# Attention front end of a fused kernel: heads grouped as 4 g + j, logits copied out of PSUM with the read-out, scores scaled as they are copied out, one tile for two sets of sums

## The chip, the cores and the metric

The kernel runs on one core of a Trainium2 chip. The metric is the device time of one execution in microseconds (us); three runs of the kernel before stand as its reference. The trace of one profiled execution gives every instruction's start and duration on TensorE (PE; PEld is its weight load), VectorE (DVE), ScalarE (ACT) and GpSimd (POOL); SP issues most of the DMA transfers, each engine's own queue is written with a q (SPq).

## The reference

Three parts follow one another: an attention between 512 tokens and 32 state rows in both directions, a mixture of experts with one expert per token, and a bilinear layer. Only the first is edited:

```
x: (B=8, H=8, S=512, D=64)   state: (8, 8, 32, 64)   scale = 1/8
xread = softmax(scale * x @ state^T) @ state      # per token, over 32 states
sread = softmax(scale * state @ x^T) @ x          # per state row, over 512 tokens
rows  = concat(xread, sread) -> (8 * 544, 512)    # heads side by side
logits = rows @ w_gate ; e = argmax ; gates also from rows @ w_output_gate
```

Both softmaxes add 1e-9 to their sums. The rows then go through the chosen expert (relu(row @ w1[e]) @ w2[e], scaled by two gates), and through ((a * b) @ w3) @ w_out with a = y @ wa, b = y @ wb.

## The kernel before, in words

**Stages.** The front (0 to 200 us of the trace) computes the attention batch by batch, converts weights given as 64-bit floats (w3 and w_out) and multiplies w3 into w_out ("fuse", TensorE). Then tokens are routed to experts, rows are gathered, and the expert and bilinear products follow.

**Layout.** The eight heads are split by `j, g = divmod(h, 2)`, so h = 2 j + g. j (0 to 3) picks one of four groups of 32 partitions, each holding the 32 state rows; g (0 or 1) picks one of two halves of columns. `load_x` brings x in four DMAs, two heads each; `load_state` and `spread_state` place the state by (j, g). The gate weights wg are loaded by two DMAs on ACT's queue.

**softmaxes(b).** x is turned by 16 transposes into four PSUM banks and copied to xT (L536, any engine or DVE). The scores psT (L548) fill two banks. Four DVE instructions (L556) copy them to sT and give the maxima m2e, joined by L561. Transposes of sT (L576) give the other direction; L580 takes its maxima per token, L581 subtracts them, L586 (ACT) takes the exponential with the scale, L588 sums it, L589 and L590 add 1e-9 and invert, and GpSimd multiplies (L593, tile an). For the state side L600 makes the bias nm2, L602 (ACT, twice) takes exponentials into a2 with sums s2, and L606 and L607 make r2 = 1/(s2 + 1e-9).

**read(b).** a2 is transposed and multiplied with x (psr, L632); L639 scales by r2, and one DMA (L643) stores the 32 state rows. an is transposed, and for each of four c (128 tokens) and two g one product pxr (L654) of 272 columns gives 256 of the read-out and 16 logits: st_d carries the state in a block-diagonal form with the state's own logits beside it. Of each bank the 256 columns are copied to xr (L140 by `cp`, any engine), and the 16 logits are copied to L (g = 0, L660) or added to it (g = 1, L662), both on DVE. Then a DMA (L663) stores 128 rows of 2 KB. The banks are those tagged C and B, two each; psr uses B too.

**Order.** The steps of a batch are traced in the order x, s, w, r, g, u, f (load of x(b+3), softmaxes(b+1), loads and conversions of w3, read(b), ...), with higher priority for s and r and lower for w. A planner lays out each engine's queue by priority from its own simulation, and picks an engine where the text says "any"; on the chip each queue runs in that order. The conversion of weights (L208 to L240) runs on ACT, DVE and GpSimd between the other work. `route` begins with L731, once all logits are in L.

Of the kernel before, what the change touches and what calls it, by code (L numbers as in the profile page):

```python
# [9 lines left out]
F32 = mybir.dt.float32  # L10
# [42 lines left out]
def tile_attention_moe_bilinear(  # L53
# [256 lines left out]
    with ExitStack() as c1:  # L310
# [12 lines left out]
        def load_x(b):  # L323

            t = xin.tile([P, H, NC_, D], F32, tag="x", name=f"x{b}")
            for j in range(NJ):
                h = slice(2 * j, 2 * j + 2)
                eng("q_x", j, "sync").dma_start(
                    out=t[:, h].rearrange("p h c d -> p h (c d)"),
                    in_=x[b, h].rearrange("h (p c) d -> p h (c d)", c=NC_),  # L330
                )
            x_t[b] = t
# [3 lines left out]

        def load_state(b, n, qs):
            for h in range(H):
                j, g = divmod(h, 2)
                qs[h % len(qs)].dma_start(  # L340
                    out=st_n[NS * j : NS * (j + 1), b : b + n, g * D : (g + 1) * D],
                    in_=state[b : b + n, h].rearrange("b n d -> n b d"),
                )
# [21 lines left out]
        if v == 5:  # L365
            load_state(0, B, (nc.scalar, nc.sync, nc.gpsimd))
            load_x(0)
        wg = one.tile([P, KD, 2 * E], F32, name="wg")
        nc.scalar.dma_start(out=wg[:, :, 0:E], in_=w_gate.rearrange("(k p) e -> p k e", p=P))
        nc.scalar.dma_start(out=wg[:, :, E:], in_=w_ogate.rearrange("(k p) e -> p k e", p=P))  # L370
        load_x(1)

        st_d = one.tile([P, B // 2, 2, NJ * D + 2 * E], F32, name="st_d")
# [6 lines left out]

        def spread_state(b, n):
            for h in range(H):
                j, g = divmod(h, 2)
# [27 lines left out]
        def of(g):  # L411
            return slice(D * g, D * (g + 1))
# [111 lines left out]
        def softmaxes(b):  # L524
            xt = x_t[b]

            xT = two.tile([P, H, S // 2], F32, tag="xT", name=f"xT{b}", bufs=kn("b_xT", 1))
            for j in range(NJ):
                t = bank((kn("t_pxT", "A")*4)[j], f"pxT{b}_{j}")
                for i in range(4):  # L530
                    c = 2 * (i % 2)
                    nc.tensor.transpose(
                        t[:, i * P : (i + 1) * P],
                        xt[:, 2 * j + i // 2, c : c + 2, :].rearrange("p c d -> p (c d)"), ident,
                    )
                cp("e_xT", j, xT[:, 2 * j : 2 * j + 2, :].rearrange("p h n -> p (h n)"), t)  # L536
# [4 lines left out]
            s2 = two.tile([P, 2], F32, tag="s2", name=f"s2{b}")  # L541
            r2 = two.tile([P, 2], F32, tag="r2", name=f"r2{b}")
# [9 lines left out]
            if kn("m2", 1):  # L552
                m2e = two.tile([P, 2, 2], F32, tag="m2e", name=f"m2e{b}")
                for g in range(2):
                    for e in range(2):
                        nc.vector.tensor_scalar(  # L556
                            sT[:, g].rearrange("p (c e n) -> p c e n", e=2, n=P)[:, :, e, :],
                            t[e][:, g * S // 2 : (g + 1) * S // 2].rearrange("p (c n) -> p c n", n=P),
                            1.0, None, op0=ALU.mult, op1=ALU.max, accum_out=m2e[:, e, g : g + 1],
                        )  # L560
                nc.vector.tensor_tensor(m2, m2e[:, 0], m2e[:, 1], op=ALU.max)  # L561
            else:
                for e in range(2):
                    cp(
                        "e_sT", e, sT.rearrange("p g (c e n) -> p g c e n", e=2, n=P)[:, :, :, e, :],
                        t[e].rearrange("p (g c n) -> p g c n", g=2, n=P),
                    )
                for g in range(2):
                    nc.vector.tensor_reduce(m2[:, g : g + 1], sT[:, g, :], axis=AX.X, op=ALU.max)
# [15 lines left out]
            av = a.rearrange("p g h n -> p (g h) n")  # L585
            nc.scalar.activation(av, av, AF.Exp, scale=SCALE)  # L586
            s1 = two.tile([P, 2 * NC_ * NJ], F32, tag="s1", name=f"s1{b}")
            nc.vector.tensor_reduce(s1, av, axis=AX.X, op=ALU.add)  # L588
            nc.vector.tensor_scalar_add(s1, s1, 1e-9)  # L589
            nc.vector.reciprocal(s1, s1)  # L590
            an = two.tile([P, 2, NC_, P], F32, tag="an", name=f"an{b}", bufs=kn("b_an", 2))
            for g in range(2):
                eng("e_an", g, "gpsimd").tensor_tensor(  # L593
                    an[:, g].rearrange("p c (j n) -> p (c j) n", n=NS), a[:, g],
                    s1[:, g * NC_ * NJ : (g + 1) * NC_ * NJ]
                    .unsqueeze(2).to_broadcast([P, NC_ * NJ, NS]),
                    op=ALU.mult,
                )
            nm2 = two.tile([P, 2], F32, tag="nm2", name=f"nm2{b}")
            nc.vector.tensor_scalar_mul(nm2, m2, -SCALE)  # L600
            for g in range(2):
# [21 lines left out]
        def read(b):  # L623
# [4 lines left out]
            for g in range(2):  # L628
                a2T = transposed(f"a2T{b}_{g}", [a2[:, g, c * P : (c + 1) * P] for c in range(NC_)], g)
                for c in range(NC_):  # L630
                    for j in range(NJ):
                        nc.tensor.matmul(  # L632
                            t[at(j), of(g)], a2T[:, c, at(j)], xt[:, 2 * j + g, c, :],
                            start=(c == 0), stop=(c == NC_ - 1),
                        )
            if b % 4 == 0:
# [6 lines left out]
            eng("q_sr", 0, "sync").dma_start(  # L643
                out=x_rows[b * R + S : (b + 1) * R, :].rearrange("n (j f) -> j n f", j=NJ), in_=sr
            )

            aT = [transposed(f"aT{b}_{g}", [an[:, g, c, :] for c in range(NC_)], 2 + g) for g in range(2)]
            xo = x_rows[b * R : b * R + S, :].rearrange("(p c) f -> c p f", c=NC_)
            for c in range(NC_):
                xr = xin.tile([P, DM], F32, tag="xr", name=f"xr{b}_{c}", bufs=kn("b_xr", 3))  # L650
                logits = L[:, b * NC_ + c]
                for g in range(2):
                    t = bank((kn("t_pxr", "CB")*8)[2 * c + g], f"pxr{b}_{c}_{g}")[:, 0 : NJ * D + 2 * E]
                    nc.tensor.matmul(t, aT[g][:, c, :], st_d[:, b % (B // 2), g], start=True, stop=True)  # L654
                    cp(
                        "e_xr", 2 * c + g, xr.rearrange("p (j g d) -> p g j d", g=2, d=D)[:, g],
                        t[:, 0 : NJ * D].rearrange("p (j d) -> p j d", d=D),
                    )
                    if g == 0:
                        nc.vector.tensor_copy(logits, t[:, NJ * D :])  # L660
                    else:
                        nc.vector.tensor_tensor(logits, logits, t[:, NJ * D :], op=ALU.add)  # L662
                eng("q_xr", c, "sync").dma_start(out=xo[c], in_=xr)  # L663

        def gates_of_state(j):
            sr = sr_t.pop(j)
# [907 lines left out]
```

## Time and profile before

| | us |
|---|---|
| three runs, median (lowest to highest) | 1168.14 (1165.36 to 1170.16) |
| profiled execution, its own time | 1171.04 |
| its span, first to last instruction | 1169.1 |
| TensorE busy | 1118.7 (96%) |
| VectorE busy | 664.0 (57%) |
| ScalarE busy | 450.7 (39%) |
| GpSimd busy | 398.2 (34%) |

A busy share is a mean over stages with different limits, so the stage that is edited is read by itself: busy time per engine in a stretch, then the instructions of one engine there by line, then what an engine waited for, then single instructions in order of time. A record's duration includes time in which the instruction is held up, and records of one engine can overlap a little.

### The profile page before, as it was taken

What the parts mean: (1) busy time and instruction counts of PE and PEld (TensorE: products, weight loads), DVE (VectorE), ACT (ScalarE), POOL (GpSimd) and SP (SyncE); (2) the same over time, 40 slices, a digit from 0 to 9 for tenths busy, and PEclk for the clock granted to TensorE, in tenths of its full rate; (3) what the DMA queues carried; (4) which work ended last, traced back from release to release, by engine and by line L of the source; (5) the groups of instructions that cost most, each with busy time, mean ns of one, the idle gap of its engine ahead of it and who ended that gap; (6) DMA issues with size and microseconds to landing.
All of it is one profiled execution on the core that took longest, in us unless ns stands there. A gap on an engine that the chain in (4) does not pass through costs nothing. (4 is left out here: it accounts for less than half of the span.)

```text
span 1169.1 us, 18224 instructions
## 1 busy us (share of the span) xinstructions
PE 1118.7 (96%) x6880; PEld 982.7 (84%) x6880; DVE 664.0 (57%) x1206; ACT 450.7 (39%) x807; POOL 398.2 (34%) x383
## 2 busy tenths in 40 slices
PE   6888998999999999999999999999999999999995
PEld 4666777999999999987888888898888889889994
DVE  4999787636464546464855547343644545463341
ACT  3778644435454545454413223121412322131121
POOL 2555326114140322132001434623543453344222
PEclk9899999999999999999999999999999999999998
DMA  7786425546566666677414645443544445343431
GB/s 227 223 254 200 160 96 209 201 153 228 187 228 211 215 216 201 233 221 242 158 35 176 248 152 199 171 174 141 205 174 160 156 180 189 135 181 132 184 127 57
DMA packets 85008, 211.55 MB, mean 181 GB/s; under 512 B 12976, under 2 KB 42672, under 8 KB 79920
## 3 DMA queue, kind: packets, MB, share of 16 engines
q1 hardware_dynamic: 62256, 167.53, 42.2%
q10 hardware_dynamic: 17024, 24.42, 5.7%
q0 software_dynamic: 5632, 18.35, 4.5%
q8 instruction: 56, 0.92, 0.3%
q14 instruction: 40, 0.33, 0.1%
HBM read 166.23 MB, written 44.04 MB: 180 GB/s over the span
## 5 line engine op out<-in xcount | busy, mean ns | idle before, releaser
L183 PE MATMUL p<-w_x,w 128*128 128x448 f32 (+1 forms) x1638 | 338.6, 360 | 0.0
L183 PEld LDWEIGHTS p<-w_x,w 128*128 128x128 f32 x1638 | 303.7, 188 | 25.4
L183 PE MATMUL py<-h,w 128*128 128x288 f32 (+1 forms) x1152 | 197.9, 329 | 3.0 <-ACT y L1087 3.0
L183 PE MATMUL ph<-x,w 128*128 128x288 f32 (+2 forms) x1248 | 196.5, 316 | 2.9 <-DVE h L1025 2.7
L183 PEld LDWEIGHTS ph<-x,w 128*128 128x128 f32 x1248 | 179.4, 188 | 15.6 <-DVE h L1025 4.4
L183 PEld LDWEIGHTS py<-h,w 128*128 128x128 f32 x1152 | 173.8, 188 | 19.2 <-ACT y L1087 4.6
L178 DVE TENSOR_TENSOR w<-raw,w 128x1024 fp32r<-128x1024 f32 x80 | 96.9, 1237 | 74.6 <-ACT w L177 72.5
L1434 POOL TENSOR_TENSOR ab<-u,s 128x448 f32<-128x448 f32 (+1 forms) x40 | 47.6, 1189 | 259.3 <-DVE u L1432 170.4
L183 PE MATMUL po<-w_wo,aa 128*128 128x512 f32 x480 | 125.3, 393 | 1.9 <-ACT aa L177 1.0
L183 PEld LDWEIGHTS po<-w_wo,aa 128*128 128x128 f32 x480 | 89.7, 188 | 18.8 <-DVE aa L178 1.7
L177 ACT CAST w<-raw 128x1024 fp32r<-128x1024 f32 x80 | 81.6, 1050 | 51.6 <-DMA raw<-in_moe_w 46.8
L177 ACT CAST ab<-ab 128x384 fp32r<-128x384 f32 (+1 forms) x40 | 19.7, 493 | 184.4 <-POOL ab L1440 174.0
L240 POOL TENSOR_TENSOR wab<-wab,wab_top 128x512 int32<-128x512 int32 x16 | 20.7, 1292 | 179.5 <-DVE wab_top L233 151.5
L183 PE MATMUL po<-w_wo,ab 128*128 128x512 f32 x336 | 79.6, 391 | 0.4 <-DVE o L1466 0.4
L183 PEld LDWEIGHTS po<-w_wo,ab 128*128 128x128 f32 x336 | 62.9, 188 | 13.9 <-DVE o L1466 0.8
L997 POOL DMA_INDIRECT xg<-x_rows,gidx x38 | 45.7, 1202 | 83.3 <-PE pxg L1003 66.7
L1437 DVE TENSOR_TENSOR u<-u,p 128x448 f32<-128x448 f32 (+1 forms) x40 | 24.3, 606 | 84.4 <-PE p L183 84.3
L1438 POOL TENSOR_TENSOR ab<-u,s 128x448 f32<-128x448 f32 (+1 forms) x40 | 48.3, 1208 | 49.2 <-DVE u L1437 49.2
L1025 DVE SCALAR_TENSOR_TENSOR h<-ph,h 128x288 fp32r<-128x288 f32 (+2 forms) x104 | 51.2, 502 | 20.8 <-ACT h L1024 20.3
L1024 ACT ACTIVATE h<-ph 128x288 fp32r<-128x288 f32 (+2 forms) x104 | 44.5, 447 | 42.6 <-PE ph L183 30.8
L183 PE MATMUL pwo<-wu,w3T 128*128 128x512 f32 x192 | 50.2, 411 | 3.4 <-POOL w3T L178 2.9
L1440 POOL TENSOR_TENSOR ab<-ab 128x448 f32<-128x448 f32 (+1 forms) x40 | 48.9, 1222 | 3.1
(291 smaller groups left out, 1441.0 us busy)
## 6 DMA issues: line engine op xcount, KB each, us to landing
w<-w_rows SPq DMA_DIRECT2D x39, 1792.0 KB
raw<-in_moe_w SPq DMA_DIRECT2D x80, 512.0 KB
x<-in_x SPq DMA_DIRECT2D x32, 256.0 KB
w_raw<-in_moe_w SPq DMA_DIRECT2D x16, 512.0 KB
x_rows<-xr SPq DMA_DIRECT2D x32, 256.0 KB
w_rows<-wh_s ACTq DMA_DIRECT2D x32, 256.0 KB
y<-y_T SPq DMA_DIRECT2D x8, 896.0 KB
w_rows<-wh_w ACTq DMA_DIRECT2D x32, 192.0 KB
```

The source lines that it names most:

```text
L177: nc.scalar.copy(hi, src)
L178: (engine or nc.vector).tensor_tensor(lo, src, hi.bitcast(F32), op=ALU.subtract)
L183: m = nc.tensor.matmul(o, l[a], r[b], start=start and i == 0, stop=stop and i == 2)
L240: nc.gpsimd.tensor_tensor(wi, wi, top, op=ALU.add)
L997: gathered = nc.gpsimd.indirect_dma_start(out=x[0:r], out_offset=None, in_=x_rows, in_offset=bass.IndirectOffsetOnAxis(ap=gidx[0:r, t - s0 ...
L1024: nc.scalar.activation(hl[0], src, AF.Relu)
L1025: nc.vector.scalar_tensor_tensor(out=hl[1], in0=src, scalar=0.0, in1=hl[0].bitcast(F32), op0=ALU.max, op1=ALU.subtract)
L1434: gpsimd(b2, u3, s5, op=ALU.add)
L1437: vector(u4, u2, p3, op=ALU.add)
L1438: gpsimd(a2, u4, s5, op=ALU.add)
L1440: gpsimd(ab[:, n : 2 * n], a2, b2, op=ALU.mult)
```

## The change

Heads are now grouped as h = 4 g + j, so the 256 columns of one g are contiguous in a row of the output. The copy out of PSUM takes all 272 columns, logits included, into a tile xr that holds two c's; logits are then added from xr in SBUF, once per two c's. The scores are multiplied by -1/8 as they are copied to sT, with minima in place of maxima; nm2 is no longer made, and the exponentials take no scale or -1. The sums of both softmaxes stand in one tile s1 of 34 columns, so 1e-9 and the reciprocal are applied once; the exponentials of the state side stand ahead of those of the token side. The state rows are stored by two DMAs, wg is loaded by four, and x's pairs of heads are loaded and turned in the order 0, 2, 1, 3.

```diff
-            for j in range(NJ):
-                h = slice(2 * j, 2 * j + 2)
+            for i in (0, 2, 1, 3):
+                h = slice(2 * i, 2 * i + 2)
...
-                j, g = divmod(h, 2)
+                g, j = divmod(h, NJ)
...
-        nc.scalar.dma_start(out=wg[:, :, 0:E], in_=w_gate.rearrange("(k p) e -> p k e", p=P))
-        nc.scalar.dma_start(out=wg[:, :, E:], in_=w_ogate.rearrange("(k p) e -> p k e", p=P))
+        for g in range(2):
+            for i, w in enumerate((w_gate, w_ogate)):
+                nc.scalar.dma_start(
+                    out=wg[D * g : D * (g + 1), :, i * E : (i + 1) * E],
+                    in_=w.rearrange("(g j d) e -> g d j e", g=2, j=NJ)[g],
+                )
...
-            for j in range(NJ):
+            for j in (0, 2, 1, 3):
                 t = bank((kn("t_pxT", "A")*4)[j], f"pxT{b}_{j}")
...
-                            xT[of(e), 2 * j + g, :], start=True, stop=True,
+                            xT[of(e), NJ * g + j, :], start=True, stop=True,
...
+                        -SCALE, None, op0=ALU.mult, op1=ALU.min, accum_out=m2e[:, e, g : g + 1],
                     )
...
+            nc.vector.tensor_tensor(m2, m2e[:, 0], m2e[:, 1], op=ALU.min)
...
-                nc.vector.tensor_reduce(m1[:, g], tv, axis=AX.X, op=ALU.max)
+                nc.vector.tensor_reduce(m1[:, g], tv, axis=AX.X, op=ALU.min)
                 nc.vector.tensor_tensor(
-                    a[:, g], tv, m1[:, g].unsqueeze(2).to_broadcast([P, NC_ * NJ, NS]),
+                    a[:, g], m1[:, g].unsqueeze(2).to_broadcast([P, NC_ * NJ, NS]), tv,
                     op=ALU.subtract,
                 )
+            s1 = two.tile([P, 2 + 2 * NC_ * NJ], F32, tag="s1", name=f"s1{b}")
+            for g in range(2):
+                nc.scalar.activation(
+                    a2[:, g, :], sT[:, g, :], AF.Exp, bias=m2[:, g : g + 1], scale=-1.0,
+                    accum_out=s1[:, g : g + 1],
+                )
             av = a.rearrange("p g h n -> p (g h) n")
-            nc.scalar.activation(av, av, AF.Exp, scale=SCALE)
-            s1 = two.tile([P, 2 * NC_ * NJ], F32, tag="s1", name=f"s1{b}")
-            nc.vector.tensor_reduce(s1, av, axis=AX.X, op=ALU.add)
+            nc.scalar.activation(av, av, AF.Exp)
+            nc.vector.tensor_reduce(s1[:, 2:], av, axis=AX.X, op=ALU.add)
             nc.vector.tensor_scalar_add(s1, s1, 1e-9)
             nc.vector.reciprocal(s1, s1)
...
-            nm2 = two.tile([P, 2], F32, tag="nm2", name=f"nm2{b}")
-            nc.vector.tensor_scalar_mul(nm2, m2, -SCALE)
-            for g in range(2):
-                nc.scalar.activation(
-                    a2[:, g, :], sT[:, g, :], AF.Exp, bias=nm2[:, g : g + 1], scale=SCALE,
-                    accum_out=s2[:, g : g + 1],
-                )
-            nc.vector.tensor_scalar_add(r2, s2, 1e-9)
-            nc.vector.reciprocal(r2, r2)
+            r2 = s1[:, 0:2]
...
-            eng("q_sr", 0, "sync").dma_start(
-                out=x_rows[b * R + S : (b + 1) * R, :].rearrange("n (j f) -> j n f", j=NJ), in_=sr
-            )
+            for g in range(2):
+                nc.sync.dma_start(
+                    out=x_rows[b * R + S : (b + 1) * R, :].rearrange(
+                        "n (g j d) -> g j n d", g=2, j=NJ
+                    )[g],
+                    in_=sr[:, of(g)],
+                )
...
+            xo = x_rows[b * R : b * R + S, :].rearrange("(p c) (g f) -> p c g f", c=NC_, g=2)
+            for c0 in range(0, NC_, 2):
+                xr = xin.tile([P, 2, 2, NJ * D + 2 * E], F32, tag="xr", name=f"xr{b}_{c0}", bufs=2)
+                for i in range(2):
+                    for g in range(2):
+                        t = bank("CB"[g], f"pxr{b}_{c0 + i}_{g}")[:, 0 : NJ * D + 2 * E]
+                        nc.tensor.matmul(
+                            t, aT[g][:, c0 + i, :], st_d[:, b % (B // 2), g], start=True, stop=True
+                        )
+                        cp("e_xr", g, xr[:, i, g], t)
+                    nc.sync.dma_start(out=xo[:, c0 + i], in_=xr[:, i, :, 0 : NJ * D])
+                nc.vector.tensor_tensor(
+                    L[:, b * NC_ + c0 : b * NC_ + c0 + 2, :], xr[:, :, 0, NJ * D :],
+                    xr[:, :, 1, NJ * D :], op=ALU.add,
+                )
```

The loop over c that this replaces is in the kernel above (L647 to L663).

## Rows read from the trace of the kernel before

**Rows 1.** The page's first line.
```profile
span 1169.1 us, 18224 instructions
```

**Rows 2.** Stretches: busy us of PE, PEld, DVE, ACT, POOL; TensorE clock, DMA share, GB/s.
```profile
40.00:128.00 88.00, 76.74 (x844) 54.55 (x826) 87.89 (x241) 66.94 (x143) 46.42 (x40) 1.00 0.74 229
128.00:146.00 18.00, 17.86 (x223) 14.52 (x222) 11.62 (x35) 14.82 (x34) 5.83 (x5) 1.00 0.32 116
...
200.00:1169.00 969.00, 947.30 (x5197) 853.82 (x5195) 497.93 (x744) 327.46 (x560) 307.61 (x283) 1.00 0.51 178
```

**Rows 3.** DVE's groups, 40 to 128 us: busy us, mean ns | idle before.
```profile
L662 DVE TENSOR_TENSOR L<-L,pxr 128x16 f32<-128x16 f32 x24 | 3.4, 152 | 0.0
L660 DVE COPY L<-pxr 128x16 f32<-128x16 f32 x24 | 3.4, 161 | 0.0
...
L561 DVE TENSOR_TENSOR m<-m2e 128x2 f32<-128x2 f32 x6 | 2.6, 435 | 0.0
L606 DVE TENSOR_SCALAR r<-s 128x2 f32<-128x2 f32 x5 | 2.4, 489 | 0.0
...
L600 DVE TENSOR_SCALAR nm<-m 128x2 f32<-128x2 f32 x6 | 1.3, 224 | 0.0
...
L607 DVE RECIPROCAL r<-r 128x2 f32<-128x2 f32 x5 | 0.8, 150 | 0.0
```

**Rows 4.** In order of time, 55 to 75 us: start, duration, engine, line, instruction.
```profile
61.46 0.16 DVE L660 COPY L<-pxr 128x16 f32<-128x16 f32 x1
...
61.55 0.68 DVE L580 TENSOR_REDUCE m<-pS 128x16 f32<-128x512 f32 x1
...
63.16 0.72 ACT L602 ACTIVATE a<-sT,nm 128x512 f32<-128x512 f32 x1
...
66.40 1.06 ACT L586 ACTIVATE a<-a 128x1024 f32<-128x1024 f32 x1
```

**Rows 5.** Instructions on tile m: ns minimum/median/maximum, first and last start.
```profile
L561 DVE TENSOR_TENSOR m<-m2e x8: 144/160/1217, 15.5 to 124.9; 128x2 f32<-128x2 f32 x8
```

**Rows 6.** In order of time, 90.4 to 92.4 us.
```profile
90.53 1.44 POOL L178 TENSOR_TENSOR wu<-wu,wu 128x512 fp32r<-128x512 f32 x1
90.77 1.22 DVE L561 TENSOR_TENSOR m<-m2e 128x2 f32<-128x2 f32 x1
...
91.99 0.24 DVE L662 TENSOR_TENSOR L<-L,pxr 128x16 f32<-128x16 f32 x2
...
92.30 0.32 PE L632 MATMUL psr<-x,a2T 128*32 128x64 f32 x8 [1.90 <-DVE L L662]
```

**Rows 7.** TensorE's waits, 40 to 128 us: total us, times, longest.
```profile
PE psr L632 <- DVE L L662: 3.3, 3, 1.9
```

**Rows 8.** ACT's groups, 40 to 128 us.
```profile
L140 ACT COPY xr<-pxr 128x256 f32<-128x256 f32 x42 | 14.7, 385 | 2.4 <-PE pxr L654 2.1
```

**Rows 9.** DMA, 40 to 128 us: a queue's packets, MB, share; then issues.
```profile
q1 hardware_dynamic: 11383, 19.98, 73.3%
...
x_rows<-xr SPq DMA_DIRECT2D x23, 256.0 KB
...
x_rows<-sr SPq DMA_DIRECT2D x5, 64.0 KB
```

**Rows 10.** In order of time: a fuse, route's first reduction, the first expert product.
```profile
121.73 5.15 PE L183 MATMUL pwo<-wu,w3T 128*128 128x512 f32 x21
...
146.31 0.44 DVE L731 TENSOR_REDUCE mx<-L 128x34 f32<-128x272 f32 x1
...
200.55 0.72 PE L183 MATMUL ph<-x,w 128*128 128x256 f32 x4
```

**Rows 11.** Instructions on tile sr: ns minimum/median/maximum of SP's issues.
```profile
L643 SPq DMA_DIRECT2D x_rows<-sr x8: 514/526/677, 33.3 to 139.8; - x8
```

**Rows 12.** In order of time, from the start.
```profile
3.97 0.41 ACTq L370 DMA_DIRECT2D wg<-in_moe_w_output_gate  x1
...
7.86 0.59 ACT L140 COPY xT<-pxT 128x512 f32<-128x512 f32 x1 [2.17 <-PE pxT L532]
```

More of the change, by code (lines that the diff above doesn't have):

```diff
@@ L325, in load_x @@
             t = xin.tile([P, H, NC_, D], F32, tag="x", name=f"x{b}")
-            for j in range(NJ):
-                h = slice(2 * j, 2 * j + 2)
-                eng("q_x", j, "sync").dma_start(
+            for i in (0, 2, 1, 3):
+                h = slice(2 * i, 2 * i + 2)
+                eng("q_x", i, "sync").dma_start(
                     out=t[:, h].rearrange("p h c d -> p h (c d)"),
@@ L382, in spread_state @@
             for h in range(H):
-                j, g = divmod(h, 2)
+                g, j = divmod(h, NJ)
                 i = b % (B // 2)
@@ L540, in softmaxes @@
             m2 = two.tile([P, 2], F32, tag="m2", name=f"m2{b}")
-            s2 = two.tile([P, 2], F32, tag="s2", name=f"s2{b}")
-            r2 = two.tile([P, 2], F32, tag="r2", name=f"r2{b}")
             t = [bank((kn("t_psT", "B")*4)[e], f"psT{b}_{e}") for e in range(2)]
@@ L549, in softmaxes @@
                             t[e][at(j), g * S // 2 : (g + 1) * S // 2], stT[e ^ g][of(e), b, at(j)],
-                            xT[of(e), 2 * j + g, :], start=True, stop=True,
+                            xT[of(e), NJ * g + j, :], start=True, stop=True,
                         )
-            if kn("m2", 1):
-                m2e = two.tile([P, 2, 2], F32, tag="m2e", name=f"m2e{b}")
-                for g in range(2):
[L555 to L559, printed above, removed]
-                        )
-                nc.vector.tensor_tensor(m2, m2e[:, 0], m2e[:, 1], op=ALU.max)
-            else:
+            m2e = two.tile([P, 2, 2], F32, tag="m2e", name=f"m2e{b}")
+            for g in range(2):
                 for e in range(2):
-                    cp(
-                        "e_sT", e, sT.rearrange("p g (c e n) -> p g c e n", e=2, n=P)[:, :, :, e, :],
-                        t[e].rearrange("p (g c n) -> p g c n", g=2, n=P),
-                    )
-                for g in range(2):
-                    nc.vector.tensor_reduce(m2[:, g : g + 1], sT[:, g, :], axis=AX.X, op=ALU.max)
+                    nc.vector.tensor_scalar(
+                        sT[:, g].rearrange("p (c e n) -> p c e n", e=2, n=P)[:, :, e, :],
+                        t[e][:, g * S // 2 : (g + 1) * S // 2].rearrange("p (c n) -> p c n", n=P),
+                        -SCALE, None, op0=ALU.mult, op1=ALU.min, accum_out=m2e[:, e, g : g + 1],
+                    )
+            nc.vector.tensor_tensor(m2, m2e[:, 0], m2e[:, 1], op=ALU.min)
             a = two.tile([P, 2, NC_ * NJ, NS], F32, tag="a", name=f"a{b}", bufs=kn("b_a", 1))
@@ L594, in softmaxes @@
                     an[:, g].rearrange("p c (j n) -> p (c j) n", n=NS), a[:, g],
-                    s1[:, g * NC_ * NJ : (g + 1) * NC_ * NJ]
+                    s1[:, 2 + g * NC_ * NJ : 2 + (g + 1) * NC_ * NJ]
                     .unsqueeze(2).to_broadcast([P, NC_ * NJ, NS]),
@@ L598, in softmaxes @@
                 )
-            nm2 = two.tile([P, 2], F32, tag="nm2", name=f"nm2{b}")
-            nc.vector.tensor_scalar_mul(nm2, m2, -SCALE)
-            for g in range(2):
-                nc.scalar.activation(
-                    a2[:, g, :], sT[:, g, :], AF.Exp, bias=nm2[:, g : g + 1], scale=SCALE,
-                    accum_out=s2[:, g : g + 1],
-                )
-            nc.vector.tensor_scalar_add(r2, s2, 1e-9)
-            nc.vector.reciprocal(r2, r2)
+            r2 = s1[:, 0:2]
             soft[b] = an, a2, r2
@@ L632, in read @@
                         nc.tensor.matmul(
-                            t[at(j), of(g)], a2T[:, c, at(j)], xt[:, 2 * j + g, c, :],
+                            t[at(j), of(g)], a2T[:, c, at(j)], xt[:, NJ * g + j, c, :],
                             start=(c == 0), stop=(c == NC_ - 1),
@@ L642, in read @@
             )
-            eng("q_sr", 0, "sync").dma_start(
-                out=x_rows[b * R + S : (b + 1) * R, :].rearrange("n (j f) -> j n f", j=NJ), in_=sr
-            )
-            aT = [transposed(f"aT{b}_{g}", [an[:, g, c, :] for c in range(NC_)], 2 + g) for g in range(2)]
[L648 to L663, printed above, removed]
@@ new lines, in read @@
+            for g in range(2):
[5 more added lines that the diff above has]
+                )
+            aT = [transposed(f"aT{b}_{g}", [an[:, g, c, :] for c in range(NC_)], 2 + g) for g in range(2)]
+            xo = x_rows[b * R : b * R + S, :].rearrange("(p c) (g f) -> p c g f", c=NC_, g=2)
+            for c0 in range(0, NC_, 2):
+                xr = xin.tile([P, 2, 2, NJ * D + 2 * E], F32, tag="xr", name=f"xr{b}_{c0}", bufs=2)
+                for i in range(2):
+                    for g in range(2):
+                        t = bank("CB"[g], f"pxr{b}_{c0 + i}_{g}")[:, 0 : NJ * D + 2 * E]
[8 more added lines that the diff above has]
+                )
```

## The prediction

> **What bounds the kernel now.** I read the page's totals first: the span is 1169.1 us [rows 1], TensorE busy 96% of it. An average over stages says nothing about an edit that touches only the attention stage, so the next view is the table by stage [rows 2]. After 200 us TensorE is busy 947 of 969 us; nothing of the change lies there, and whatever the front of the kernel gains or loses should be handed on whole. From 40 to 128 us the picture is another: VectorE (DVE) is busy 87.89 of 88 us, TensorE 76.74, ScalarE (ACT) 66.94, GpSimd (POOL) 46.42. There DVE's queue has no hole; TensorE has 88 - 76.7 = 11.3 us of them. This stretch holds the read-out of six of the eight batches. From 128 to 146 TensorE is full again (17.86 of 18 us): a fuse of the later weights starts at 121.73 us, ahead of the last batch's remainder [rows 10]. Routing starts at 146.31 us, when the last logits are there, and the first expert product runs at 200.55 us [rows 10]; this chain of 54 us is not edited, and moves as a block with its start.
>
> So the question is how much DVE time in 40 to 128 us goes, and whether TensorE, whose work stays the same, can use it: at most its 11.3 idle us.
>
> **The change part by part.** All of it on DVE first. A record's length overstates what a small instruction takes from the queue: an L660 copy starts at 61.46 us, its record lasts 0.16, and the next instruction starts at 61.55 [rows 4]; it took 0.09 and overlapped the next by some 0.08.
>
> 1. *Logits.* 24 copies L660 and 24 additions L662 leave the stretch: 3.4 + 3.4 = 6.8 us by records [rows 3], 48 x 0.09 = 4.3 us by starts. I take 4.3.
>
> 2. *nm2, and s2/r2 as part of s1.* L600 (6), L606 (5) and L607 (5) go: 1.3 + 2.4 + 0.8 = 4.5 us by records [rows 3], 16 x 0.09 = 1.4 us if each is only a start. L600 and L607 are short, 11 x 0.09 = 1.0. L606 has a mean of 489 ns on two columns, so it is mostly held up; 5 x (0.489 - 0.08) = 2.0. I take 3.0. Part of that hold-up may pass to whoever stands behind it. L589 and L590 work on 34 instead of 32 columns: nothing.
>
> 3. *The new logit additions.* One over two c's, 12 in the stretch, both inputs in SBUF. No such row exists; the nearest is L561, tiny and with both inputs in SBUF: mean 435 ns in the stretch [rows 3], minimum 144, median 160, longest 1217 ns [rows 5]. The longest is in rows 6: L561 starts at 90.77 us, just after a GpSimd instruction over 128x512 (90.53, 1.44 us), and ends as that one does, at 91.99. The price lies between 12 x 0.09 = 1.1 and 12 x (1.217 - 0.08) = 13.6 us; by L561's mean it is 12 x (0.435 - 0.08) = 4.3 us, which I take.
>
> What the trace shows there the Trainium skill states as a rule ("SBUF — State Buffer", section "Who interferes with whom"): a VectorE instruction with two SBUF inputs contends with a GpSimd instruction that reads SBUF, and the later one is blocked until the earlier ends, whereas one with at most one SBUF input (outside the two-port modes) is not. By that rule the old additions, with one input in PSUM, are free of it (152 ns mean, as rows 3 have it) and the new ones are not; the rule speaks against this part, and its worst case is a rival below.
>
> DVE's sum: 4.3 + 3.0 - 4.3 = 3.0 us less. Ends: 5.7 (all removed at 0.09) - 13.6 = 7.9 us more, and 11.3 (all records whole) - 1.1 = 10.2 us less.
>
> 4. *PSUM banks.* A bank of the read-out now comes free with its one copy. Before, it also waited for L660 or L662 in DVE's full queue: TensorE's products psr waited 3.3 us for L662 [rows 7], 1.9 of them at once, behind the blocked L561 [rows 6]. Between 0 and 3.3 us; since TensorE then meets the next wait on DVE, I take 1.0.
>
> 5. *Copies of 272 instead of 256 columns* on ACT: 42 of 385 ns [rows 8] grow by a sixteenth, 42 x 0.024 = 1.0 us on an engine with 21 idle us [rows 2]. Hidden; if ACT were the bound, 1.0 us. Which of ACT and DVE copies is left open by the text ("any").
>
> 6. *Order of the exponentials.* a2's stand ahead of a's in the text now. In the trace they already run so: 63.16 against 66.40 us [rows 4]. s1's addition now waits for both; a2's are done by then. Nothing, and at most one exponential of 0.72 us per batch, 8 x 0.72 = 5.8 us, if it came to wait; GpSimd's multiplication (an) stands behind it, and behind that TensorE's transposes.
>
> 7. *Pairs of heads 0, 2, 1, 3.* The first scores need two pairs transposed instead of one, the same 16 transposes in all; while the second pair is turned TensorE is at work anyway. 0 to one copy of xT per batch (0.59 us on ACT [rows 12], 3.5 us over six batches); taken at 0. Negation by -SCALE with a minimum instead of 1.0 with a maximum, and the swapped subtraction, keep count and shape: 0.
>
> 8. *DMA.* Each xr row goes out as two pieces of 1 KB, not one of 2 KB; sr goes in two DMAs of 256-byte pieces. In the stretch that is (23 + 5) x 128 = 3584 more packets [rows 9]. The queue's 11383 packets took 73.3% of 16 x 88 us [rows 9], 91 ns each; at that price 3584 x 0.091 / 16 = 20.4 us of all engines, and the share would go from 0.74 to 0.97; with bytes alone counting, 0. I take it as covered by the free quarter. SP issues one more sr per batch, 0.53 us [rows 11], in front of the loads of weights behind it: 4 us of SP's time in all, not on the path. If that cover is gone, conversions of weights come late, on engines that then have room.
>
> 9. *wg in four DMAs.* Two more issues on ACT's queue, 0.41 us each [rows 12] and so 0.8 in all, before ACT's first copy, which waits 2.17 us idle for TensorE [rows 12]. Hidden.
>
> **Sum.** 3.0 + 1.0 = 4.0 us earlier at 128 us, so at 146, at 200 and at the end. The profiled execution took 1171.04 us (span 1169.1, 1.9 around it), 2.9 above the median of the three runs, 1168.14. Against its own time: 1171.0 - 4.0 = 1167.0; on the median, 1168.1 - 4.0 = 1164.1 us.
>
> **The rivals.**
> *A, the queue gains whole records.* The blocked parts vanish and TensorE fills its holes: 10.2 us, just inside the 11.3 available. 1168.1 - 10.2 = 1157.9. For it: DVE has no gap in 88 us. Against: the overlap in rows 4, and rows 6, where the blocked time belongs to GpSimd and not to the instruction.
> *B, the new additions are held up by GpSimd.* Place: the 12 of 40 to 128 us. With a share of 46.42 / 88 = 53% GpSimd is usually at work, in instructions of 1.1 to 1.4 us. At L561's longest each takes 1.14: 13.6 - 7.3 = 6.3 us more, 1174.4. It decides from 7.3 / 12 = 0.61 us per addition; below that the edit gains. For it: the rows of L561 and L606. Against: L561's median is 160 ns, so most meet nothing. The rule of the Trainium skill's page on SBUF, told under 3, gives this outcome where every addition meets a long GpSimd instruction; the rows of L561 show that for few of them.
> *C, hidden anyway.* DVE's time goes, but the order that is planned for the low-priority weight conversions fills it, and TensorE reaches 121.73 us with the same idle time: 1168.1. For it: conversions are in the same stretch and needed only later. Against: they are a fixed amount of work, so a shorter queue ends earlier.
>
> **How the numbers follow.** Forecast 40% (its own range 1159 to 1168), A 27%, B 20%, C 13%. The measurement tells about 0.5%, 5.8 us, from no change: faster means below 1162.3. A is there, and of the forecast's own spread about a quarter: 0.27 + 0.11 = 0.38. Slower is B: 0.20. Within 0.5%: 0.29 + 0.13 = 0.42. The range goes from a little below A to a little above B, 1155 to 1176: any replanned order of so many small instructions can add or take a few us to each case.
>
> **What would show it.** Right: L606, L607, L600 and L660 gone, 16 additions on L with durations between 0.15 and 1.2 us and a mean near 0.4; DVE still full between 40 and some 124 us; psr no longer waiting for L; route's first reduction at about 142 instead of 146.31 us, and the first expert product as much earlier as that. Wrong: DVE showing holes in the stretch (then another engine bounds it); the first reduction earlier but the first expert product not; a large share of the xr copies on DVE; waits for loads of weights several times today's; additions near 1.1 us; or a difference that arises behind 200 us, which would mean that the front's time is not handed on.

## The result, and the profile after

The change is slower: 1177.79 us (median of 6 runs, 1175.44 to 1179.55) against 1169.31 us of the kernel before beside it, a ratio of 1.0074, 95% interval [1.0057, 1.0091]. The profiled execution took 1175.44 us, 4.4 us more than that of before; so the traces show about half of the 8.5 us between the medians. These runs lie up to 4 us to either side of their kernel's median, so what the other half consists of no trace here shows.

The page's first line, and the table by stage (columns as in [rows 2]):

```profile
span 1173.7 us, 18149 instructions
```

```profile
40.00:128.00 88.00, 74.65 (x825) 51.93 (x818) 83.77 (x169) 66.43 (x145) 46.97 (x39) 0.98 0.72 220
128.00:146.00 18.00, 18.00 (x223) 15.06 (x222) 11.31 (x29) 10.82 (x25) 2.06 (x2) 1.00 0.37 125
146.00:200.00 54.00, 47.59 (x252) 36.73 (x252) 43.56 (x135) 24.77 (x45) 23.17 (x17) 0.97 0.34 122
200.00:1173.00 973.00, 953.49 (x5221) 859.24 (x5219) 502.24 (x747) 330.25 (x563) 309.83 (x286) 0.99 0.52 179
```

Against [rows 2]: VectorE is less busy in 40 to 128 us (83.77 for 87.89), as the change intends, but TensorE is less busy too (74.65 for 76.74). The freed time became holes on VectorE, and TensorE was busy 2.1 us less.

VectorE's new additions in the stretch (busy us, mean ns, idle before), then all of them (minimum, median, maximum ns):

```profile
L655 DVE TENSOR_TENSOR L<-xr 128x32 f32<-128x32 f32 x11 | 7.3, 665 | 2.3 <-ACT xr L140 2.3
```

```profile
L655 DVE TENSOR_TENSOR L<-xr x16: 177/388/1244, 42.2 to 150.8; 128x32 f32<-128x32 f32 x16
```

The 48 short instructions on logits [rows 3] are gone, and so are L600, L606 and L607 of before; the new addition costs 665 ns on average. TensorE's waits in the stretch (total us, times, longest):

```profile
PE pS L570 <- DVE sT L558: 4.9, 4, 2.3
PE psr L624 <- ACT a2T L140: 3.3, 1, 3.3
PE paT L606 <- DVE L L655: 1.8, 1, 1.8
```

The wait of psr for the logits [rows 7] is gone; as much is now waited for a copy on ACT. In order of time (start, duration, idle before in brackets), that wait:

```profile
79.43 0.66 ACT L239 ACTIVATE w<-w_raw 128x512 int32<-128x512 uint32 x1 [2.57 <-DMA w_raw<-in_moe_w]
79.99 0.37 ACT L140 COPY xr<-pxr 128x272 f32<-128x272 f32 x1
80.26 1.08 ACT L140 COPY a2T<-pa2T 128x512 f32<-128x512 f32 x2
...
80.40 0.19 DVE L655 TENSOR_TENSOR L<-xr 128x32 f32<-128x32 f32 x1 [2.33 <-ACT xr L140]
...
80.90 0.49 PE L624 MATMUL psr<-x,a2T 128*32 128x64 f32 x20 [3.26 <-ACT a2T L140]
```

ACT stood for 2.57 us before a weight conversion whose data had not come; queued behind it were the copies that VectorE (2.33 us) and TensorE (3.26 us) wanted. It is a matter of what stands behind what. Routing and the first expert product start at:

```profile
151.48 0.43 DVE L726 TENSOR_REDUCE mx<-L 128x34 f32<-128x272 f32 x1
...
204.57 0.64 PE L183 MATMUL ph<-x,w 128*128 128x256 f32 x4
```

That is 5.2 and 4.0 us later than in [rows 10]. Of the 4.6 us between the two spans, 4.0 stand ahead of the expert products in this pair of traces; that isn't so for every new order, as r2 shows below.

### The profile page after: what moved, and what is told of

The parts are those of the page before. It is cut to its first block, busy times and chain, and to the rows that moved or that the text cites. A ratio compares the mean times of both kernels' runs of the same rounds, so it can differ in the third digit from the quotient of the medians.

```text
span 1173.7 us, 18149 instructions
## 1 busy us (share of the span) xinstructions
PE 1121.5 (96%) x6880; PEld 984.9 (84%) x6880; DVE 667.0 (57%) x1133; ACT 449.8 (38%) x808; POOL 398.2 (34%) x383
```

## The experiments

The order of each engine's queue is not in the kernel's text: it is laid out when the kernel is built, by a planner that models the times, and so is the engine of the copies that the text leaves open ("any"). An edit can therefore move instructions that it doesn't touch. "Order" below means both, the places in the queues and the engines of these copies. The expectations number their theories; they come to: the parts of the change cost by themselves (the additions held up on SBUF, the smaller store pieces, the place of the exponentials, the pairs of heads), or the newly laid-out order costs. The last six tell these apart.

All ratios are to the kernel before, run beside each. "In order" is the share of the first 1300 TensorE, 330 VectorE and 330 ACT entries that stand in the same succession as in before, counted in the queues as they were laid out. The traces bear out the rows with 1, with "that of" and e2; the shares between were not read from traces.

| kernel | in order (PE, DVE, ACT) | median us | ratio [95%] |
|---|---|---|---|
| the change | .88, .75, .76 | 1177.79 | 1.0074 [1.0057, 1.0091] |
| e1_add_gpsimd | .87, .75, .74 | 1172.63 | 1.0034 [1.0019, 1.0049] |
| e2_rows_2k | .88, .75, .76 | 1180.01 | 1.0084 [1.0061, 1.0108] |
| e3_logits_as_before | .90, .67, .81 | 1172.77 | 1.0030 [1.0012, 1.0047] |
| e4_sums_scale | .87, .72, .78 | 1173.31 | 1.0034 [1.0015, 1.0053] |
| n1_exps_ahead | 1, 1, 1 | 1167.66 | 0.9996 [0.9975, 1.0017] |
| n2_pairs_order | .93, .67, .82 | 1172.47 | 1.0037 [1.0019, 1.0055] |
| n5_order_read_first | 1, 1, 1 | 1167.35 | 0.9995 [0.9979, 1.0010] |
| r1_regroup_only | .85, .60, .75 | 1178.59 | 1.0102 [1.0073, 1.0132] |
| r2_regroup_g_outer | .86, .60, .73 | 1175.69 | 1.0067 [1.0046, 1.0088] |
| f2_after_g_outer | .87, .72, .75 | 1174.37 | 1.0051 [1.0035, 1.0067] |
| f1_after_gpsimd_g_outer | .86, .74, .74 | 1176.38 | 1.0064 [1.0042, 1.0086] |
| s2_joint_only | .90, .76, .83 | 1177.85 | 1.0078 [1.0057, 1.0098] |
| p1_joint_in_order | 1, 1, 1 | 1165.74 | 0.9983 [0.9966, 1.0001] |
| p2_before_in_s2_order | that of s2 | 1196.85 | 1.0250 [1.0229, 1.0271] |
| p3_regroup_in_order | 1, 1, 1 | 1166.41 | 0.9988 [0.9970, 1.0007] |
| p4_after_in_order | 1, 1, 1 | 1166.13 | 0.9982 [0.9966, 0.9998] |
| p5_e4_in_order | 1, 1, 1 | 1166.43 | 0.9984 [0.9971, 0.9998] |
| p9_before_in_r2_order | that of r2 | 1178.65 | 1.0087 [1.0069, 1.0106] |

**Parts of the change, in the planner's order**

*e1: the additions of logits on GpSimd.*

```
-                nc.vector.tensor_tensor(
+                nc.gpsimd.tensor_tensor(
                     L[:, b * NC_ + c0 : b * NC_ + c0 + 2, :], ...
```

> The changed kernel with one edit: the 16 additions of the logits run on GpSimd instead of VectorE; nothing is left out. Before: 1169.3 us, changed: 1177.8. Theory 1 (the additions: 9.2 us of VectorE's queue by their records, held up by GpSimd, and 2.3 us at once in which the queue stands behind a copy on ScalarE) expects the loss back, 1167 to 1170, with VectorE full in the stretch again. Theory 2 (the smaller pieces of the stores make the loads of weights late, and ScalarE waits 8.9 instead of 5.7 us for them) expects no change, 1176 to 1179. Theory 3 (the whole order was laid out anew, and no single edit is to blame) expects something between, without a clear place.

1.0034, better than the change. It looked as if the additions were half of the loss; but this kernel has an order of its own, and f1 below did not repeat it.

*e2: both halves of xr side by side, stored in pieces of 2 KB instead of 1 KB.*

```
-                    nc.sync.dma_start(out=xo[:, c0 + i], in_=xr[:, i, :, 0 : NJ * D])
+                    nc.sync.dma_start(out=xo[:, c0 + i], in_=xr[:, i].rearrange("p g f -> p (g f)")[:, 2 * E : 2 * E + DM])
```

> The changed kernel with the logits of g = 0 ahead of its 256 columns and those of g = 1 behind, so that a row of xr is 512 numbers in one piece and each store row is one piece of 2 KB again; copies, additions and counts stay. Theory 1 (additions on VectorE): no change, 1176 to 1179. Theory 2 (pieces): most of the loss back, 1169 to 1172, and ScalarE's wait for loads of weights back to about 6 us in the stretch. Theory 3: any change without a change of that wait.

1.0084, as the change, and ScalarE still waits 9.2 us for loads of weights (8.9 in the change): the pieces of xr's stores are not the cause. Its queues stand exactly as the change's. The state rows keep their smaller pieces here.

*e3: the change with the logits taken from PSUM as before.*

```
-                        cp("e_xr", g, xr[:, i, g], t)
+                    cp("e_xr", g, xr[:, g * NJ * D : (g + 1) * NJ * D], t[:, 0 : NJ * D])
+                    if g == 0:
+                        nc.vector.tensor_copy(logits, t[:, NJ * D :])
+                    else:
+                        nc.vector.tensor_tensor(logits, logits, t[:, NJ * D :], op=ALU.add)
```

> The changed kernel with the logits taken from PSUM by VectorE as before (32 copies, 32 additions), copies of 256 columns, one tile of 512 columns per c, stores in 2 KB pieces; grouping, scaling and the joint sums stay changed. Theories 1 and 2 both expect the loss back and part 2 of the prediction as a gain, 1165 to 1168. If the grouping, the order of pairs or the joint sums cost the time: 1174 or more. Theory 3: 1168 to 1178.

*e4: before, with the scale by the evacuation and the joint sums only.*

```
-                            1.0, None, op0=ALU.mult, op1=ALU.max, accum_out=m2e[:, e, g : g + 1],
+                        -SCALE, None, op0=ALU.mult, op1=ALU.min, accum_out=m2e[:, e, g : g + 1],
...
-            nc.vector.tensor_scalar_add(r2, s2, 1e-9)
-            nc.vector.reciprocal(r2, r2)
+            r2 = s1[:, 0:2]
```

> The kernel before with two edits alone: scores scaled by the copies out of PSUM (no nm2) and one tile for both sides' sums, exponentials of the state side ahead. Grouping, logits and stores as before. The prediction's part 2 expects 3.0 us less, 1166. If the joint sums are the loss (the multiplication on GpSimd and r2 waiting for each other): 1173 or more. Theory 3 (a new order costs by itself): 1171 to 1178 with no instruction to point at.

e3 and e4 came out alike, 1.0030 and 1.0034. e4 takes 24 instructions from VectorE, adds nothing, and is slower all the same: less work on the full engine did not help.

**Single edits of before**

*n1: the state side's exponentials ahead of the tokens' in the text. n5: another order of tracing the stages.*

```
+            nm2 = two.tile([P, 2], F32, tag="nm2", name=f"nm2{b}")
+            nc.vector.tensor_scalar_mul(nm2, m2, -SCALE)
...
             av = a.rearrange("p g h n -> p (g h) n")
```

```
-    'order': 'xswrguf'
+    'order': 'xsrwguf'
```

> The kernel before with the state side's bias and exponentials (L600, L602) traced ahead of the token side's exponential and nothing else: the same instructions, another order. Three versions of the change that keep its joint sums (additions on GpSimd; logits as before; sums and scaling alone) all came out 0.30 to 0.34% (some 4 us) slower than before. Theory 4 (the exponentials' place in the order is those 4 us) expects 1172 to 1174. Theory 3 (the order of before is a good one among its neighbours, and any new order costs some us) expects 1170 to 1174 too, and the same of the two runs after this one. If neither: 1169, as before.

> The kernel before with read(b) traced ahead of the loads and conversions of w3 of the same batch (the letters w and r of the order swapped). Same instructions, another order, and no part of the change. Theory 3: 1170 to 1174. Theory 4: 1169, as before.

Both are meant as other orders, and both came out of the planner with the queues of before, entry by entry. They tell nothing of another order; they show how equal two kernels with the same one are, 0.9996 and 0.9995.

*n2: the pairs of heads in the order 0, 2, 1, 3, and nothing else.*

```
-            for j in range(NJ):
+            for j in (0, 2, 1, 3):
```

> The kernel before with x's pairs of heads loaded and turned in the order 0, 2, 1, 3 and nothing else; with the old grouping this order serves no purpose. Same instructions, another order. Theory 3: 1170 to 1174. Theory 4: 1169, as before.

1.0037 with the same instructions. The queues did change; the copy of xT that the text gives to VectorE, that of pair 2, comes second in a batch by this edit and not third.

*r1: the regrouping as 4 g + j alone, with its DMAs (wg in four, sr in two) and pairs. r2: r1 with pairs in natural order and the scores' loops turned round, so that the first scores need one pair only.*

```
-                j, g = divmod(h, 2)
+                g, j = divmod(h, NJ)
...
-                            xT[of(e), 2 * j + g, :], start=True, stop=True,
+                            xT[of(e), NJ * g + j, :], start=True, stop=True,
```

```
-            for j in range(NJ):
-                for g in range(2):
+            for g in range(2):
+                for j in range(NJ):
```

> The kernel before with the grouping 4 g + j alone (with it: pairs 0, 2, 1, 3, wg in four DMAs, the state rows in two DMAs, plain copies of 256 columns); logits, scaling and sums as before. The prediction's parts 7 to 9 expect 1169. Theory 4: 1169. Theory 3: 1170 to 1174.

> The grouping 4 g + j alone, as in the run that came out 1.02% slower (1178.6 us), but with the scores computed g first and j second, and x's pairs loaded and turned in the order 0, 1, 2, 3: now every pair of heads that is turned feeds four score products at once, as it did before. Theory 5 (the regrouped scores have to wait for two pairs; the order of pairs alone cost 0.37% under the old grouping, where it has the same effect) expects 1168 to 1172. Theory 6 (the DMAs of the grouping: wg in four, state rows in two) expects 1178, no change. Theory 3 (the layout of the order decides, whatever the reason): anything from 1168 to 1180.

1.0102 and 1.0067: the regrouping alone seems to cost more than the whole change.

*f2: the change with r2's turn. f1: f2 with the additions on GpSimd (both edits stand above).*

> The whole change with the same edit: scores g first, pairs 0, 1, 2, 3. Theory 5: 1170 to 1174, since what the additions on VectorE cost (some 5 us by the run with them on GpSimd) stays. Theory 6: 1178.

> The whole change with both edits: the logits' additions on GpSimd, and scores g first with pairs 0, 1, 2, 3. Theories 1 and 5 together expect the forecast's gain at last, 1163 to 1168. Without theory 5: 1172.6, as with the additions on GpSimd alone.

1.0051 and 1.0064: here GpSimd's additions gain nothing, where e1's seemed to gain 0.4%.

*s2: before with the joint tile of sums alone, 16 VectorE instructions fewer.*

```
-            nc.vector.tensor_scalar_add(r2, s2, 1e-9)
-            nc.vector.reciprocal(r2, r2)
+            r2 = s1[:, 0:2]
```

> The kernel before with the joint sums alone (one tile s1 of 34 columns, L606 and L607 gone, exponentials of the state side ahead; nm2 and the scale stay). The exponentials' place alone made no difference. The prediction's part 2 expects some 2.3 us less, 1166. If the joint sums are what made sums and scaling together 0.34% slower: 1172 to 1174.

1.0078. The parts do not add up: sums alone 0.78%, sums and scale 0.34%, regrouping 1.02%, all three 0.30% (e3). What they share is a new order. Several expectations were missed: r1 and s2 are slower than any of their theories allowed, r2 is slower than theory 5 had it, and e3 and f1 did not bring the loss back as theories 1, 2 and 5 had it.

**The order held fast**

Each instruction was given the place in its queue that its counterpart has in another kernel, by dependences that order without a semaphore; copies left open got the same engine as there. In the traces the first 330 instructions of VectorE and of ScalarE in p3 stand exactly as in before, and in p9 exactly as in r2.

```
+def _queue(tc):
+    by = {i.name: i for i in tc.nc.cur_bb.bb.instructions}
+    for v in _QUEUES.values():
+        for a, b in zip(v, v[1:]):
+            tc.add_manual_dep(by[f"I-{b}"], f"I-{a}", mybir.DependencyInfo(
+                mybir.DependencyClass.NoSync, mybir.DependencyReason.DATA), reason="queue order")
...
+        v = next(anys) if v == "any" else v
```

> The kernel before with the joint tile of sums alone (16 VectorE instructions fewer), as in s2_joint_only, but with every engine's queue held to the order that the kernel before has; s2_joint_only in the order that the planner laid out for it came to a ratio of 1.0078. Theory 3 (what costs is the queue order that the planner lays out anew, not the work that the edit changes): the loss is gone, 0.997 to 1.001 of the kernel before, 1165 to 1169 us. Rival (the joint sums themselves cost, by the wait of the one addition for both sides' exponentials): it stays at 1.005 to 1.010, some 1174 to 1180 us.

> The kernel before, every instruction of it, with its queues held to the order that the planner laid out for s2_joint_only; the 16 instructions that s2_joint_only has not stand right behind the addition and the reciprocal of the same batch. Theory 3: the order alone costs, 1.005 to 1.010, 1173 to 1180 us. Rival (the edit costs, not the order): 0.998 to 1.002.

> The whole change, with its queues held to the order of the kernel before, each instruction in the place of the one that it stands for (the addition of logits in the place of the second addition of the same pair of blocks). In the planner's own order the change is at 1.0074. Theory 3: 0.995 to 1.001, 1162 to 1169 us, and if the sum of the prediction holds in a fixed order, 1164. Rival (the parts of the change cost by themselves, the additions of logits first): 1.004 to 1.009.

> The kernel before with the scale by the evacuation and the joint tile of sums (24 VectorE instructions fewer), with its queues held to the order of the kernel before; in the planner's own order it is at 1.0034. Theory 3: 0.995 to 1.000, 1162 to 1168 us. Rival: 1.002 to 1.005.

By the ratios to before p1, which has the text of s2, is 0.95% (11.1 us) faster than s2; the whole change (p4) is 0.92% (10.8 us) faster than in the planner's order; p5 is faster than e4 by 0.50% (5.8 us). Each median stands a little below before's. In p4 VectorE's fixed copy of xT is the third of a batch, as in before; in the change it is the second. p2, the reverse, is at 1.025, beyond its theory's range; its 16 hand-placed instructions may be part of that, so it proves the sign only together with p9.

> The kernel before, with its heads as they are, in the queue order that the planner laid out for r2_regroup_g_outer (grouping 4 g + j, pairs in natural order; 1.0067 in that order). Each instruction of before has one counterpart there, so nothing had to be placed by hand, as 16 instructions of p2 had. Theory 3 (the order costs): 1.004 to 1.010, 1173 to 1180 us. Rival (the regrouping itself costs 0.67%): 0.998 to 1.002.

> r2_regroup_g_outer in the queue order of the kernel before; the eight second stores of the state's read-out and the two second loads of the gates' weights stand right behind the first ones. Theory 3: 0.999 to 1.002, 1167 to 1170 us, for the regrouping alone takes no engine work away. Rival (the regrouping itself costs): 1.004 to 1.009.

These complete a square without hand-placed instructions of weight:

| | before's order | r2's order |
|---|---|---|
| before's heads | 1 | 1.0087 [1.0069, 1.0106] |
| regrouped heads | 0.9988 [0.9970, 1.0007] | 1.0067 [1.0046, 1.0088] |

The order costs 0.8 to 0.9% in either row; the regrouping costs nothing in either column. The two kernels whose order was held are one faster and one slower than their text in its own order, so the holding itself is not what costs. The theory that the order costs is shown, the theories that blame a part are not needed.

How p4 differs from the change in the trace, stretches of 10 us from 60 to 110 us (busy PE, PEld, DVE, ACT, POOL); the change first, then p4:

```profile
60.00:70.00 10.00, 7.67 (x110) 6.42 (x111) 10.00 (x27) 9.09 (x19) 4.87 (x6) 1.00 0.65 210
70.00:80.00 10.00, 7.14 (x59) 4.14 (x57) 8.06 (x19) 5.12 (x14) 5.47 (x4) 1.00 0.91 282
80.00:90.00 10.00, 9.10 (x117) 7.31 (x118) 8.41 (x17) 10.00 (x24) 4.98 (x4) 0.83 0.85 271
90.00:100.00 10.00, 7.63 (x85) 5.16 (x84) 9.93 (x22) 6.33 (x16) 6.40 (x7) 1.00 0.71 217
100.00:110.00 10.00, 9.78 (x100) 6.39 (x100) 10.00 (x17) 7.85 (x17) 3.45 (x3) 1.00 0.52 150
```

```profile
60.00:70.00 10.00, 9.99 (x121) 7.35 (x119) 10.00 (x19) 8.55 (x19) 6.11 (x7) 1.00 0.59 174
70.00:80.00 10.00, 8.24 (x123) 5.75 (x123) 9.82 (x26) 7.87 (x18) 5.15 (x5) 1.00 0.96 332
80.00:90.00 10.00, 10.00 (x88) 7.81 (x87) 9.41 (x23) 8.50 (x21) 6.03 (x7) 1.00 0.68 227
90.00:100.00 10.00, 7.16 (x97) 5.53 (x96) 9.88 (x18) 7.70 (x17) 4.43 (x5) 0.83 0.74 222
100.00:110.00 10.00, 9.98 (x138) 6.83 (x137) 9.96 (x26) 8.04 (x18) 6.67 (x5) 1.00 0.74 237
```

In these 50 us TensorE works 45.4 us in p4 and 41.3 in the change. VectorE is at 8.06 and 8.41 in the change's second and third stretch: the engine that was to be relieved waits there with TensorE. p4 by stage, then where it waits (TensorE and VectorE, 40 to 128 us), its additions (in 40 to 128 us, then all), and its milestones:

```profile
40.00:128.00 88.00, 78.05 (x827) 55.88 (x826) 83.13 (x185) 67.07 (x145) 46.88 (x40) 0.96 0.73 230
```

```profile
PE psT L625 <- ACT xT L214: 2.6, 2, 2.5
PE pxT L611 <- DVE a L649: 2.5, 2, 2.2
PE paT L680 <- ACT a2T L214: 1.8, 1, 1.8
```

```profile
DVE s L662 <- ACT a L661: 1.7, 1, 1.7
DVE w_top L302 <- ACT w_top L299: 1.6, 2, 0.9
```

```profile
L729 DVE TENSOR_TENSOR L<-xr 128x32 f32<-128x32 f32 x12 | 7.1, 588 | 0.1
```

```profile
L729 DVE TENSOR_TENSOR L<-xr x16: 122/193/1264, 43.5 to 145.1; 128x32 f32<-128x32 f32 x16
```

```profile
145.59 0.44 DVE L800 TENSOR_REDUCE mx<-L 128x34 f32<-128x272 f32 x1
...
199.12 0.60 PE L257 MATMUL ph<-x,w 128*128 128x256 f32 x3
```

A single trace is good to some 3 us here: in n1 and n5, with the queues of before, the first expert product starts at 197.68 and 199.07, in before at 200.55 [rows 10]. So p4's 0.7 and 1.4 us earlier prove nothing by themselves; its ratio does, narrowly.

Where another order loses is not one place. s2 and p1, one text in two orders, part in 60 to 100 us (TensorE 31.4 and 35.6 busy us), where s2's TensorE has these waits:

```profile
PE psr L629 <- DVE a2T L140: 2.6, 1, 2.6
PE psr L629 <- DVE L L659: 1.7, 2, 1.5
PE pxr L651 <- DVE L L657: 1.6, 1, 1.6
PE pxr L651 <- DVE L L659: 1.5, 1, 1.5
```

p9 starts routing at 147.37 us, 1.1 later than before, and loses in routing: the stage from 146 to 200 us, where TensorE has 49.06 busy us in before, and TensorE's waits there:

```profile
146.00:200.00 54.00, 45.26 (x238) 35.08 (x238) 41.47 (x134) 21.02 (x37) 21.10 (x15) 0.94 0.33 119
```

```profile
PE pxg L1078 <- DMA xg<-x_rows,gidx: 4.3, 2, 3.3
PE pwo L258 <- ACT w3T L252: 2.7, 1, 2.7
```

Its first expert product starts at 203.93 us, 3.4 later than before, and 3.8 of the 7.2 us between the spans (1176.3 and 1169.1) come behind it. In r2, the kernel whose order p9 has, all of the traced loss does: routing and the first expert product start no later than in before, and yet its span is 1173.9 us. TensorE there, with its wait for VectorE's h, then 210 to 230 us in before and in r2:

```profile
146.26 0.43 DVE L737 TENSOR_REDUCE mx<-L 128x34 f32<-128x272 f32 x1
...
199.61 0.63 PE L183 MATMUL ph<-x,w 128*128 128x256 f32 x4
...
202.43 2.49 PE L183 MATMUL pwo<-wu,w3T 128*128 128x512 f32 x10
...
217.72 13.25 PE L183 MATMUL ph<-x,w 128*128 128x256 f32 x96 [2.38 <-DVE h L1031]
```

```profile
210.00:230.00 20.00, 20.00 (x148) 18.95 (x148) 14.42 (x27) 12.34 (x24) 2.24 (x2) 1.00 0.55 176
```

```profile
210.00:230.00 20.00, 17.62 (x136) 17.39 (x135) 11.39 (x22) 9.33 (x17) 2.70 (x2) 0.91 0.59 176
```

Part of the fuse (pwo) now stands behind the first expert product, and TensorE has holes where before has none. An order can cost in the part of the kernel that the change doesn't touch.

## Why the prediction was wrong

The step that failed is the sum's last sentence, "4.0 us earlier at 128 us, so at 146, at 200 and at the end". It takes it that everything which is not edited keeps its place. The prediction knew that the order is laid out anew, but gave it a width ("can add or take a few us to each case") and no term. The term is 1.0074 / 0.9982, 0.92% or 10.8 us, larger than the gain that it was added to, and not of both signs here: the kernels in all ten orders that the planner laid out anew are slower than before, by 0.30 to 1.02%. Where the same work was run in both orders, the new one costs 0.37 to 0.95% (2.5% in p2, where instructions were placed by hand).

The rest, by its own points, read in p4 where the order is fixed:

1 and 2, *instructions removed*: gone as told. With 3, VectorE's busy time in the stretch falls from 87.89 to 83.13 us, 4.8 us, where 3.0 were forecast in queue time. The two are not the same measure, since records overlap. It is not handed on whole: VectorE now has 4.9 us of holes, and the kernel gains 2.1 us by its ratio. TensorE is busy 1.3 us more in the stretch (78.05 for 76.74), but at a granted clock of 0.96 for 1.00, so this need not be work gained. The text named this ("VectorE showing holes in the stretch, then another engine bounds it"): the next waits are for ACT's copies and exponentials.

3, *the new additions*: 588 ns each in p4 and 665 in the change, where 435 were taken from L561. By the prediction's formula 12 x (0.588 - 0.08) = 6.1 us and not 4.3; mis-sized by 1.8, within its bounds. With the median at 193 ns and the longest at 1264, rival B's mechanism is there, at a mean that stays below its point of decision (0.61 us and the 0.08 of overlap, so 0.69 by record). At 665 ns twelve of them take 7.0 of the 7.3 us freed; by that sum it makes the gain nothing and cannot make 8.5 us of loss. The Trainium skill ("SBUF — State Buffer", section "Who interferes with whom") has such an addition wait for the end of a GpSimd instruction that reads SBUF and began before it; the traces agree. Of the 32 additions of the change and p4, 15 take 522 to 1264 ns; each starts while a GpSimd instruction runs and ends 0.04 to 0.05 us after it. The other 17 take 122 to 193 ns: 15 of them meet no GpSimd instruction, one starts 0.03 us ahead of one, and one meets only its last 0.07 us. The longest, in p4:

```profile
91.82 1.28 POOL L314 TENSOR_TENSOR w<-w,w_top 128x512 int32<-128x512 int32 x1
91.89 1.26 DVE L729 TENSOR_TENSOR L<-xr 128x32 f32<-128x32 f32 x1
```

4, *PSUM banks*: psr no longer waits for L, in the change or in p4. The next wait is about as long: 3.3 us for ACT's a2T in the change, 2.6 for ACT's xT in p4. Of the 1.0 us nothing shows: p1 and p5, which have the sums alone or with the scale, gain as much as p4 (0.9983, 0.9984 and 0.9982), so as far as these intervals tell the gain is that of part 2, where 3.0 us were forecast.

5, *wider copies*: 404 ns (42 in the stretch, p4) for 385, 0.8 us in all, hidden.

6, *exponentials*: nothing; n1, with this move alone, came out in before's order.

7, *pairs*: no cost shows in a fixed order, since p4 has them and is at 0.9982. n2's 0.37% came with its new order.

8, *DMA*: 3756 packets more in p4's stretch (15139 for 11383), where 3584 were forecast, at a share of 72.3 for 73.3%:

```profile
q1 hardware_dynamic: 15139, 20.05, 72.3%
```

It costs nothing that shows, as taken; e2 says the same of xr's pieces.

9, *wg in four DMAs*: nothing; p3 and p4 have them.

So the mechanism of the sum was right in sign and about half in size, 2.1 us [0.2, 4.0] for 4.0, and was outweighed five times by a cost that isn't in the diff. What in an order costs stays open. p1 and s2, p4 and the change show that it is queue places and the engines of open copies, and the rows above show waits behind late loads, behind VectorE's copies and behind ACT's conversions; no run moved one of these alone. The premise that what the front gains or loses is handed on whole does not hold for r2's order, where the traced loss arises behind the first expert product (2.5 us of it is fuse that now stands there). Why before's order is better than every neighbour's was not tried either.

One thing goes with the order in all runs: TensorE's granted clock. Its mean over the runs of a kernel is 0.991 for before and 0.989 to 0.992 for the six kernels with before's order; for the thirteen others it is 0.979 to 0.988. The clock has two levels in these traces, 2.4 GHz and 1.2 (1.00 and 0.50). In the change it is at 0.50 from 82 to 84 us, after TensorE was busy for 7.67 and 7.14 us of the two 10 us from 60 to 80. As an estimate, the span times (1 - mean clock) is 15.9 us of full clock not granted in the change and 10.4 to 10.9 in before, some 5 of the 8.5 us if TensorE were the bound throughout. No run held the clock, so it stays open how much of this is a cost of its own and how much the sign of longer waits.

The fastest versions are p1, p4 and p5, all within 0.06% of each other and 0.16 to 0.18% below before; only p4's and p5's intervals exclude no change, by 0.02%.

## What to carry to other kernels

Where a planner lays out the queues, compare the order of the edited kernel with the old one before pricing the edit: an edit that keeps it is worth its sum, one that loses it carries a second cost, here several times the gain. Test parts of a change in a fixed order, for in a free one they are not additive, and parts that gain a little come out as losses. Look behind the edited stage as well, since a new order can lose there. And time freed on the fullest engine is worth only what the next waiter lets through, here some 2 of 4.8 us.

## What was not expected of the hardware

A small addition with both inputs in SBUF varies tenfold in one kernel, 122 to 1264 ns in p4: it is short, or it ends with the GpSimd instruction that it met. Its mean in the stretch, 588 ns, is three times its median, so its price must be read as a mean over many and not from one row.
